# Thresholds and epsilon on another engine, shorter GpSimd pieces, paired V products, and a new order in a fused attention and two-layer expert kernel

## The chip, the cores and the metric

The kernel runs on one core of one Trainium2 chip. The metric is the device time of one execution in microseconds. A core has TensorE (matrix products, PE in the profile, with its weight loads apart as PEld), VectorE (DVE), ScalarE (ACT), GpSimd (POOL) and SyncE (SP), which issues most of the transfers. Each engine works through its own queue in order and waits there on semaphores of the others.

## The reference

```python
def _attn_ref(q, k, v, tau):                     # (4, 8, 576, 64) each
    scores = scale * np.matmul(q, k.transpose(0, 1, 3, 2))
    thresh = np.max(scores, axis=-1, keepdims=True) - tau
    scores = np.where(scores >= thresh, scores, -1000000000.0)
    attn = np.exp(scores - np.max(scores, axis=-1, keepdims=True))
    attn = attn / (np.sum(attn, axis=-1, keepdims=True) + 1e-09)
    return np.matmul(attn, v)
def _moe_ref(x, w_in, w_out):                    # (2304, 512), (512, 2048), (2048, 512)
    h = x @ w_in
    return (h - np.tanh(h)) @ w_out
def _moe2_ref(x, w_gate, w_output_gate, w1, w2): # 8 experts of 512 x 1024
    # each token goes to the expert of its largest logit:
    out[mask] = gate_w[mask, None] * eom[mask, e, None] * (np.maximum(x[mask] @ w1[e], 0.0) @ w2[e])
```

The attention's output, as 2304 tokens of 512, goes through the dense layer, and its result through the routed experts.

## The kernel before

The work has three stages. In the attention stage (0 to about 470 us) 32 units run one after another: 4 batches, two halves of the queries (`half` 0 with two tiles of 128 queries, `half` 1 with two and a merged third) and four pairs of heads. A unit is made of blocks of 128 queries by 576 keys, 144 in all. For a block TensorE makes the scores (L1085, or L1096 in the first eight units); VectorE copies them out of PSUM, negated and scaled, with their minimum (`em`, L1106); ScalarE makes the exponential (`e`, L1109); and VectorE masks it by the threshold, multiplies and sums in one instruction, the masked product (L1122, scalar_tensor_tensor with two inputs in SBUF). The threshold itself (`tb`, L1118) is one small addition of tau to the minima of a query tile, both heads at once. TensorE then transposes the block (L1138), ScalarE copies the transposes to `eth` and `elh`, and TensorE multiplies with V (L1193, half of the array's columns for each head), a burst of ten products for a unit, in two groups (`BURST`). The row sums `rs` get epsilon added (L1160) and are inverted (L1162), spread to `rb` (L1171, L1168), transposed into `rp`, and multiplied into the result `xf` (L1212). The high half of it, `xh`, is rounded on ScalarE or GpSimd (`round_to`) and the low half, `xl`, is a subtraction on GpSimd (`rest`).

Numbers are kept as a high and a low part in the format fp32r. `rest` makes all low parts: of K (`kst`), of q (`ql`), of the dense layer's weights (`wi`, `wo`, after the conversion from 64-bit numbers on L681 to L694), of the hidden values (`gl`), and of `xl`. On GpSimd a subtraction of more than `HALVE` = 400 columns is cut in two.

Steps of the dense layer (L743 into `ph`, L777 into `x`, with L756 to L766 between them) run beside the attention as soon as a chunk of 256 tokens is ready, and fill TensorE to about 720 us. The experts (L1750, L1637 and L1783) follow.

Buffers are rings: a tile of a tag with n buffers waits for the last use of the tile n before it. `EMN, EN, ETN, RBN` are the ring sizes of `em`, `e`, `eth` with `elh`, and `rb`.

The order of the instructions on each engine is set when the kernel is built. Every instruction is added to a planner with a duration in ns and a due time; `TAU` = 2600 ns is the due-time step of a block. In the main part the due times are replaced by a packed list of priorities, `URGENCY`, one for each instruction, and a greedy list schedule with the planned durations gives the order. The planner knows of a port that VectorE's instructions marked `port=True` share with GpSimd's.

## Time and profile before

| | before |
|---|---|
| time, median of 3 runs | 970.16 us (969.92 to 971.55) |
| the profiled execution | 971.04 us, of which the span of instructions is 969.2 |
| TensorE busy | 940.4 us (97%) |
| VectorE busy | 727.5 us (75%) |
| ScalarE busy | 551.1 us (57%) |
| GpSimd busy | 346.0 us (36%) |
| mean granted TensorE clock | 0.998 |

Busy time is the union of an engine's instructions; an instruction that waits for a resource after its start counts as busy. Matrix products are pipelined, and their recorded ends are modelled, so a busy TensorE isn't one at its peak. In a row of a group stand the line, the engine, the operation, the tiles written and read, the shapes, the count, then the busy time in us, the mean length in ns, the idle time of the engine just before these instructions in us, and what ended it.

### The profile page before, as it was taken

The page shows a single profiled execution, that of the slowest core. Times are in us where ns is not written, and L with a number is a line of the kernel's source. Part 1 is how long each engine was busy: PE and PEld are TensorE (multiplying, and loading weights), DVE is VectorE, ACT ScalarE, POOL GpSimd, SP SyncE. Part 2 cuts the span into 40 slices and gives each one's busy share as a digit, 9 for nine tenths or more (in the row PEclk, how much of TensorE's full clock was granted, in tenths as well). Part 3 has the DMA queues.
Part 4 walks back from the last instruction along what each step waited for, and adds up shares of the span by engine and source line. Part 5 has one row for each costly group of instructions (what it writes and reads, how often), then busy time and mean ns, then how long its engine had stood idle before and what let it go on. Part 6 is the DMA issues. An engine that isn't in the chain of part 4 may idle for free.

```text
span 969.2 us, 18499 instructions
## 1 busy us (share of the span) xinstructions
PE 940.4 (97%) x6636; PEld 806.5 (83%) x6636; DVE 727.5 (75%) x1812; ACT 551.1 (57%) x1142; POOL 346.0 (36%) x434
## 2 busy tenths in 40 slices
PE   8899889999999999999999999999999999999996
PEld 4556667888888888888899888888888899999996
DVE  7999999898789877857268668888676777646630
ACT  5888777777778767757445444344343434435421
POOL 1368548884667754434210101011012302213101
PEclk9999999999999999999999999999999999999999
DMA  9264645565664662451595366476854876655600
GB/s 268 102 204 150 195 139 183 170 206 169 198 215 160 193 244 86 132 182 45 180 364 175 118 189 158 130 169 137 266 177 144 271 229 229 193 169 165 214 14 32
DMA packets 71604, 168.70 MB, mean 174 GB/s; under 512 B 32382, under 2 KB 33022, under 8 KB 65616
## 3 DMA queue, kind: packets, MB, share of 16 engines
q1 hardware_dynamic: 67872, 157.41, 51.3%
q0 software_dynamic: 3200, 9.77, 2.9%
q8 instruction: 54, 0.88, 0.4%
q14 instruction: 46, 0.38, 0.1%
q10 hardware_dynamic: 432, 0.26, 0.1%
HBM read 125.99 MB, written 35.45 MB: 167 GB/s over the span
## 4 chain that ended last, share of the span: by engine, by line
PE 81%; DVE 14%; issue 2%; ACT 1%; DMA 1%; POOL 0%; POOLq 0%; DVEq 0%; ACTq 0%
PE x L777 20%; PE ph L743 20%; PE ph L1750 9%; PE py L1637 8%; PE sp L1085 5%; PE pv L1193 5%; DVE em L1122 5%; PE pt L1138 4%; DVE em L1106 3%; PE py L1783 2%; DVE ct L691 1%; PE pt L1682 1%; PE ph L1388 1%; DVE ct L694 1%; DVE tb L1118 1%
## 5 line engine op out<-in xcount | busy, mean ns | idle before, releaser
L743 PE MATMUL ph<-xh,wi 128*128 128x256 f32 x1152 | 178.1, 286 | 1.2 <-DVE u L766 1.1
L777 PE MATMUL x<-wo,gh 128*128 128x512 f32 x576 | 167.7, 404 | 0.0
L743 PEld LDWEIGHTS ph<-xh,wi 128*128 128x128 f32 x1152 | 156.3, 188 | 10.4 <-DVE u L766 3.1
L1122 DVE SCALAR_TENSOR_TENSOR em<-em,tb,e 128x576 f32<-128x576 f32 x144 | 142.4, 1003 | 8.0 <-ACT e L1109 5.0
L1109 ACT ACTIVATE e<-em,mx 128x576 f32<-128x576 f32 x144 | 110.8, 774 | 46.1 <-DVE em L1106 43.3
L1106 DVE TENSOR_SCALAR_CACHE_REDUCE em<-sp 128x576 f32<-128x576 f32 x144 | 107.6, 749 | 36.9 <-PE sp L1085 31.0
L556 POOL TENSOR_SCALAR gh<-u 128x512 fp32r<-128x512 f32 x52 | 38.4, 739 | 220.2 <-DVE u L766 168.5
L777 PEld LDWEIGHTS x<-wo,gh 128*128 128x128 f32 x576 | 99.0, 189 | 16.4 <-issue 1.3
L756 ACT ACTIVATE u<-ph 128x512 f32<-128x512 f32 x72 | 43.0, 598 | 94.2 <-PE ph L743 89.9
L764 DVE SCALAR_TENSOR_TENSOR w<-w,u 128x512 f32<-128x512 f32 x72 | 53.9, 748 | 53.6 <-ACT w L760 53.3
L743 PE MATMUL ph<-xl,wi 128*128 128x256 f32 x576 | 93.5, 284 | 0.0
L1138 PE MATMUL pt<-ident,em 128*128 128x128 f32 x576 | 84.3, 276 | 7.6 <-DVE em L1122 5.2
L554 ACT ACTIVATE eth<-pt 128x512 f32<-128x512 f32 (+1 forms) x160 | 84.6, 548 | 12.5 <-PE pt L1138 11.7
L777 PE MATMUL x<-wo,gl 128*128 128x512 f32 x288 | 90.6, 401 | 0.0
L1138 PEld LDWEIGHTS pt<-ident,em 128*128 128x128 f32 x576 | 65.6, 141 | 22.9 <-ACT eth L554 6.5
L743 PEld LDWEIGHTS ph<-xl,wi 128*128 128x128 f32 x576 | 79.6, 189 | 1.0
L1085 PE MATMUL sp<-kst,qh 128*128 128x288 f32 (+2 forms) x252 | 73.7, 311 | 2.9 <-DVE em L1106 2.8
L1193 PE MATMUL pv<-eth,vt 128*64 128x256 f32 (+1 forms) x512 | 71.6, 414 | 0.9 <-ACT elh L554 0.9
L1619 POOL DMA_INDIRECT out_dram<-o,ids x23 | 24.4, 1059 | 130.9 <-ACT o L1615 127.6
L1755 ACT ACTIVATE hh<-ph 128x320 fp32r<-128x320 f32 (+2 forms) x56 | 22.7, 420 | 83.2 <-PE ph L1750 82.9
L574 DVE TENSOR_TENSOR w<-wraw,w 128x512 fp32r<-128x512 f32 x98 | 65.5, 688 | 5.7 <-ACT w L554 4.3
L1085 PE MATMUL sp<-kst,ql 128*128 128x288 f32 (+2 forms) x252 | 68.0, 293 | 0.0
(380 smaller groups left out, 2003.7 us busy)
## 6 DMA issues: line engine op xcount, KB each, us to landing
wraw<-in_w_dram SPq DMA_DIRECT2D x60, 512.0 KB, 4.5
wi<-wsv SPq DMA_DIRECT2D x17, 1024.0 KB, 5.8
wo<-wsv SPq DMA_DIRECT2D x17, 1024.0 KB, 6.2
craw<-in_w_in_dram SPq DMA_DIRECT2D x14, 512.0 KB, 5.1
craw<-in_w_out_dram SPq DMA_DIRECT2D x14, 512.0 KB, 3.8
kr<-in_kT_dram SPq DMA_DIRECT2D x24, 288.0 KB, 4.6
wsv<-wi SPq DMA_DIRECT2D x6, 1024.0 KB, 4.6
wsv<-wo SPq DMA_DIRECT2D x6, 1024.0 KB, 5.9
```

The lines of the kernel that those rows point to most:

```text
L554: return sc.add("ACT", act(n, psum), due, lambda: nc.scalar.activation(dst(), src(), AF.Copy), r, w)
L574: return sc.add(eng, dve(n, psum) + 5 if eng == "DVE" else pool_tt(n), due, lambda: e.tensor_tensor(out=dst(), in0=src(), in1=hi().bitcast ...
L743: nc.tensor.matmul(ph.t[:, j, :], wi.t[:, w_, cc * CH + j * P:cc * CH + (j + 1) * P], x_.t[:, cc, :], start=(n == 0 and cc == 0), stop=(n ...
L777: nc.tensor.matmul(x2b[c, half][t].t, g_.t[:, j, t * P:(t + 1) * P], wo.t[:, w_, j * DM:(j + 1) * DM], start=(first and n == 0 and j == 0) ...
L1085: nc.tensor.matmul(sp.t[:, kb_, o:o + w], q_.t[:, q0:q0 + P], kb.t[:, hh, c0:c0 + w], start=(i == 0), stop=(i == len(todo) - 1),)
L1106: sc.add("DVE", 665, d, lambda ev=ev, sp=sp, mx=mx: nc.vector.tensor_scalar(out=ev().rearrange("p (a b) -> p a b", a=2), in0=sp.t[:, :, 0: ...
L1109: sc.add("ACT", 667, d + 800, lambda e=e, ev=ev, mx=mx: nc.scalar.activation(e.t, ev(), AF.Exp, bias=mx(), scale=-1.0), [(em, h), (m2, h)] ...
L1122: sc.add("DVE", 729, d + TAU, lambda ev=ev, tb=tb, e=e, col=col: nc.vector.scalar_tensor_tensor(out=ev(), in0=ev(), scalar=tb(), in1=e.t, ...
L1138: nc.tensor.matmul(pt.t[:, kt, :], em.t[:, c0:c0 + P], ident, is_transpose=True, start=(kt == 0), stop=(kt == 3))
L1193: nc.tensor.matmul(pvf()[h * D:(h + 1) * D], vb_.t[:, k, :], eth[h].t[:, kt, 0:n] if kt < 4 else elh.t[:, 0:n], start=(kt == 0), stop=(kt ...
L1637: nc.tensor.matmul(py[k].t[:, 0:cap], wx()[:, k * P:(k + 1) * P], x_.t[:, 0:cap], start=(f == 0 and n == 0), stop=(f == 7 and n == 2))
L1750: nc.tensor.matmul(ph.t[:, 0:cap], wx()[:, cc * P:(cc + 1) * P], x_.t[:, cc, 0:cap], start=(n == 0 and cc == 0), stop=(n == 2 and cc == 3))
```

## The change

- `thr` and `eps` go from "D" to "A": the 80 thresholds and the 32 epsilon additions are ScalarE's (activation Identity with a bias) and no longer VectorE's.
- `rest` on GpSimd cuts a subtraction into pieces of at most 144 columns (`FINE`) where its due time is before 150 us (`FINE_T`), and of at most 288 after that.
- `products` is a new function that issues the V products and all that follows them. For `half` 0 of batches 2 and 3 it is called once for two units: their twenty products are one instruction group on TensorE, into two halves of one PSUM bank. All other units call it alone.
- The ring of `e` has 2 buffers in place of 3, and that of `rb` 5 in place of 3.
- The planner's durations of some instructions change (335 to 343 for L685 and L688, 602 to 607, 665 to 678, 729 to 745, 400 to 570 and the like), which changes no instruction, and the list `URGENCY` is another one.

```diff
@@ -47,10 +47,13 @@
 ROUNDS = 24
 PORT = True
 HOLD = 160
-HALVE = 400
+HALVE = 288
+FINE = 144
+FINE_T = 150e3
 FULL = 8
 EARLY = 4
-EMN, EN, ETN, RBN = 5, 3, 2, 3
+EMN, EN, ETN, RBN = 5, 2, 2, 5
+PAIRED = 2
 BURST = (3, 2)
 WARMUP = 9
 NHH = 12
@@ -61,8 +64,8 @@
 ENGINES = {
     "conv_h": "A", "conv_l": "P", "conv_lb": "D", "ga_h": "P", "ga_l": "PPPD", "gb_h": "DP", "gb_l": "D", "k_h": "A",
     "k_l": "P", "q_h": "A", "q_l": "P", "p_h": "A", "p_l": "D", "p_h2": "A",
-    "x_h": "AP", "x_l": "P", "w_h": "AD", "w_l": "D", "w_l0": "D", "f_h": "A", "thr": "D", "eps": "D", "r_2": "DA",
-    "r_3": "PD", "clamp": "D", "bot": "A", "sum": "D",
+    "x_h": "AP", "x_l": "P", "w_h": "AD", "w_l": "D", "w_l0": "D", "f_h": "A", "thr": "A", "eps": "A", "r_2": "DA",
+    "r_3": "PD", "clamp": "D", "bot": "A", "sum": "D", "xm": "D",
 }
 LAG = {
     ("ACT", "DVE"): 150, ("ACT", "PE"): 260, ("ACT", "POOL"): 172, ("DVE", "ACT"): 130, ("DVE", "PE"): 256,
@@ -560,15 +562,17 @@
 
     def rest(cls, n, due, dst, src, hi, r, w, psum=False):
         eng = pick(cls) if cls in ENGINES else cls
-        if eng == "POOL" and n > HALVE:
+        if eng == "POOL":
+            np_ = -(-n // (FINE if due < FINE_T else HALVE))
+
             def part(k):
                 a, b, h_ = dst(), src(), hi().bitcast(F32)
                 m = a.shape[1]
-                cut = slice(0, (m + 1) // 2) if k == 0 else slice((m + 1) // 2, m)
+                cut = slice(m * k // np_, m * (k + 1) // np_)
                 nc.gpsimd.tensor_tensor(out=a[:, cut], in0=b[:, cut], in1=h_[:, cut], op=ALU.subtract)
 
-            for k in range(2):
-                o = sc.add("POOL", pool_tt(n // 2) + 110, due, lambda k=k: part(k), r, w)
+            for k in range(np_):
+                o = sc.add("POOL", pool_tt(n // np_), due, lambda k=k: part(k), r, w)
             return o
         e = nc.vector if eng == "DVE" else nc.gpsimd
         return sc.add(eng, dve(n, psum) + 5 if eng == "DVE" else pool_tt(n), due, lambda: e.tensor_tensor(
@@ -1115,11 +1119,11 @@
                 sc.add("ACT", 187, d + 801, lambda m2=m2, t2=t2, nt=nt: nc.scalar.activation(
                     t2.t[:, 0:nt], m2.t[:, 0:nt], AF.Identity, bias=tau_t), [m2, tau_m], [t2])
             else:
-                sc.add("DVE", 75, d + 801, lambda m2=m2, t2=t2, nt=nt: nc.vector.tensor_scalar(
+                sc.add("DVE", 133, d + 801, lambda m2=m2, t2=t2, nt=nt: nc.vector.tensor_scalar(
                     out=t2.t[:, 0:nt], in0=m2.t[:, 0:nt], scalar1=tau_t, scalar2=None, op0=ALU.add), [m2, tau_m], [t2])
             for h, d, mx, tb, ev, e in tl:
                 col = 4 if merged else 2 * h + qt
-                sc.add("DVE", 729, d + TAU, lambda ev=ev, tb=tb, e=e, col=col: nc.vector.scalar_tensor_tensor(
+                sc.add("DVE", 745, d + TAU, lambda ev=ev, tb=tb, e=e, col=col: nc.vector.scalar_tensor_tensor(
                     out=ev(), in0=ev(), scalar=tb(), in1=e.t, op0=ALU.is_le, op1=ALU.mult,
                     accum_out=rs.t[:, col:col + 1]), [t2, e], [(em, h), (rs, col)], port=True)
             dl = d
@@ -1157,15 +1161,15 @@
             sc.add("ACT", 200, ds, lambda: nc.scalar.activation(
                 rs.t[:, 0:nr], rs.t[:, 0:nr], AF.Identity, bias=eps_t), (), [rs])
         else:
-            sc.add(eng, 75 if eng == "DVE" else 220, ds, lambda: e_.tensor_scalar(
-                out=rs.t[:, 0:nr], in0=rs.t[:, 0:nr], scalar1=1e-9, scalar2=None, op0=ALU.add), (), [rs])
-        sc.add("DVE", 81, ds, lambda: nc.vector.reciprocal(out=rs.t[:, 0:nr], in_=rs.t[:, 0:nr]), (), [rs])
+            sc.add(eng, 110 if eng == "DVE" else 220, ds, lambda: e_.tensor_scalar(
+                out=rs.t[:, 0:nr], in0=rs.t[:, 0:nr], scalar1=1e-9, scalar2=None, op0=ALU.add), (), [rs], port=True)
+        sc.add("DVE", 92, ds, lambda: nc.vector.reciprocal(out=rs.t[:, 0:nr], in_=rs.t[:, 0:nr]), (), [rs])
         rbs = []
         for qt in range(2 + half):
             rb = buf("sm", "rb", RBN, [P, P])
             rbs.append(rb)
             if qt == 2:
-                sc.add("POOL", 400, ds + 260, lambda rb=rb: nc.gpsimd.tensor_scalar(
+                sc.add("POOL", 570, ds + 260, lambda rb=rb: nc.gpsimd.tensor_scalar(
                     out=rb.t, in0=blk, scalar1=rs.t[:, 4:5], scalar2=None, op0=ALU.mult), [rs], [rb])
             else:
                 sc.add("ACT", act(P), ds + 260, lambda rb=rb, qt=qt: nc.scalar.activation(
@@ -1181,50 +1185,77 @@
         round_to("p_h2", n, dl + 500, lambda: elh.t[:, 0:n], lambda: plf()[:, 0:n], slots, [elh], True)
         if half:
             round_to("p_h2", D, dl + 500, lambda: elh.t[D:P, 256:320], lambda: plf()[D:P, 320:384], slots, [elh], True)
-        xf = buf("ep", "xf", 2, [P, 320])
-        dl += TAU
+        waiting.append((ui, dl + TAU, eth, elh, rbs))
+        if half or b < PAIRED or hp % 2:
+            products(waiting)
+            del waiting[:]
+        return dl + 5 * TAU
+
+    waiting = []
+
+    def products(todo):
+
+        dl = todo[-1][1]
         pv = buf("ps_v", "pv", 1, [P, 4, P])
-        pvf = lambda: pv.t.rearrange("p a b -> p (a b)")[:, 0:n]
...
+        xfs, runs = [], []
+        for i, (ui, _, eth, elh, rbs) in enumerate(todo):
+            b, half, hp = units[ui]
+            n = 320 if half else 256
+            vb_ = vts[b, hp]
+            pvf = lambda i=i, n=n: pv.t.rearrange("p a b -> p (a b)")[:, 256 * i:256 * i + n]
+
+            def pairs_(kts, pvf=pvf, vb_=vb_, eth=eth, elh=elh, n=n):
+                for kt in kts:
+                    for h in range(2):
+                        nc.tensor.matmul(
+                            pvf()[h * D:(h + 1) * D], vb_.t[:, 2 * kt + h, :],
+                            eth[h].t[:, kt, 0:n] if kt < 4 else elh.t[:, 0:n], start=(kt == 0), stop=(kt == 4))
+
+            k0_ = 0
+            for g in BURST if len(todo) == 1 else ():
+                sc.add("PE", (538 if half else 432) * g, dl, lambda k0_=k0_, g=g, pairs_=pairs_: pairs_(range(k0_, k0_ + g)),
+                       [vb_] + [elh] * (k0_ + g == 5) + eth, [(pv, i)], mode=1)
+                k0_ += g
+            runs.append((pairs_, [vb_, elh] + eth))
+            if len(todo) > 1 and i:
+                sc.add("PE", 432 * 10, dl, lambda: [f(range(5)) for f, _ in runs],
+                       [x for _, r in runs for x in r], [(pv, 0), (pv, 1)], mode=1)
+        for i, (ui, _, eth, elh, rbs) in enumerate(todo):
+            b, half, hp = units[ui]
+            n = 320 if half else 256
+            pvf = lambda i=i, n=n: pv.t.rearrange("p a b -> p (a b)")[:, 256 * i:256 * i + n]
+            xf = buf("ep", "xf", 2, [P, 320])
+            xfs.append(xf)
+            round_to("bot", n, dl + 1200, lambda xf=xf, n=n: xf.t[:, 0:n], pvf, [(pv, i)], [xf], True)
+        for (ui, _, eth, elh, rbs), xf in zip(todo, xfs):
+            b, half, hp = units[ui]
+            n = 320 if half else 256
+            d = dl + 2 * TAU
+            rp = buf("ps_v", "pv", 1, [P, 4, P])
+            rpf = lambda rp=rp: rp.t.rearrange("p a b -> p (a b)")
+            for qt, rb in enumerate(rbs):
+                if qt < 2:
+                    sc.add("PE", 109, d, lambda qt=qt, rb=rb, rp=rp: nc.tensor.transpose(rp.t[:, qt, :], rb.t, ident), [rb], [(rp, qt)])
+                else:
+                    sc.add("PE", 120, d, lambda qt=qt, rb=rb, rp=rp: nc.tensor.matmul(
+                        rp.t[:, qt, 0:D], rb.t, sel, start=True, stop=True), [rb], [(rp, qt)])
...
+                round_to("x_h", m, d + 1500, hi, src, [xf], [(xh, reg)])
+                rest("x_l", m, d + 1500, lambda xl=xl, r=r, m=m, hp=hp: xl.t[:, hp, r:r + m], src, hi,
+                     [xf, (xh, reg)], [(xl, reg)])
+                o += m
 
     starts = []
     k = 0
```

## Rows read from the trace of the kernel before

**Rows 1.** Stretches: PE, PEld, DVE, ACT, POOL busy us (instructions), granted clock, DMA.
```profile
0.00:160.00 160.00, 140.76 (x954) 93.14 (x955) 151.25 (x382) 122.55 (x246) 87.76 (x116) 1.00 0.55 172
160.00:480.00 320.00, 319.02 (x2267) 270.04 (x2266) 248.95 (x554) 227.29 (x471) 183.16 (x241) 1.00 0.51 168
480.00:740.00 260.00, 258.93 (x1878) 230.05 (x1877) 195.04 (x622) 113.32 (x238) 31.27 (x36) 1.00 0.62 185
740.00:970.00 230.00, 221.70 (x1543) 213.32 (x1542) 132.27 (x255) 87.90 (x188) 43.79 (x42) 0.99 0.53 171
```

**Rows 2.** Chain that ended last, by line, 0 to 160 and 160 to 480 us.
```profile
by line: DVE em L1122 27.6%; DVE em L1106 19.8%; issue 6.1%; DVE ct L691 5.4%; DVE ct L694 5.0%; DVE tb L1118 4.4%; DMA craw<-in_w_in_dram 4.0%; PE ph L743 3.6%; DVE ct L685 2.8%; PE pv L992 2.6%; DVE ct L688 2.5%; ACT e L1109 1.8%; PE pt L
...
by line: PE x L777 24.0%; PE ph L743 23.6%; PE sp L1085 16.2%; PE pv L1193 15.3%; PE pt L1138 11.3%; PE pv L1177 1.7%; PE pv L1208 1.2%; DVE em L1122 1.1%; issue 1.1%; DVE w L764 0.6%; PE pv L1210 0.5%; DVE em L1106 0.5%; ACT e L1109 0.5%; 
```

**Rows 3.** VectorE, groups by line and form, 0 to 160 us: busy, mean ns.
```profile
L1122 DVE SCALAR_TENSOR_TENSOR em<-em,tb,e 128x576 f32<-128x576 f32 x59 | 58.5, 997 | 0.9
...
L1106 DVE TENSOR_SCALAR_CACHE_REDUCE em<-sp 128x576 f32<-128x576 f32 x60 | 44.6, 747 | 5.0 <-PE sp L1096 4.8 <-PE sp L1085 0.2
...
L1118 DVE TENSOR_SCALAR tb<-mx,tau_t 128x2 f32<-128x2 f32 x27 | 9.7, 361 | 0.2
...
L685 DVE TENSOR_SCALAR ct<-ct 128x512 f32<-128x512 f32 x13 | 7.5, 576 | 1.0 <-ACT ct L681 1.0
...
L688 DVE TENSOR_SCALAR ct<-ct 128x512 uint32<-128x512 uint32 x13 | 7.4, 572 | 0.1
...
L1160 DVE TENSOR_SCALAR rs<-rs 128x4 f32<-128x4 f32 x8 | 1.8, 231 | 0.1
...
L1160 DVE TENSOR_SCALAR rs<-rs 128x5 f32<-128x5 f32 x5 | 1.5, 302 | 0.0
...
L1118 DVE TENSOR_SCALAR tb<-mx,tau_t 128x1 f32<-128x1 f32 x5 | 1.0, 197 | 0.0
```

**Rows 4.** VectorE, timeline at 55 to 58 us: start, length.
```profile
55.26 1.23 DVE L1122 SCALAR_TENSOR_TENSOR em<-em,tb,e 128x576 f32<-128x576 f32 x1
...
56.42 1.28 DVE L1122 SCALAR_TENSOR_TENSOR em<-em,tb,e 128x576 f32<-128x576 f32 x1
...
58.31 0.41 DVE L685 TENSOR_SCALAR ct<-ct 128x512 f32<-128x512 f32 x1
```

**Rows 5.** GpSimd, timeline at 55 to 58 us.
```profile
55.83 2.46 POOL L568 TENSOR_TENSOR ql<-qr,qh 128x256 fp32r<-128x256 f32 x2
```

**Rows 6.** Views of single lines: duration ns min/median/max; L574 from 0 to 160 us.
```profile
L1118 DVE TENSOR_SCALAR tb<-mx,tau_t x80: 178/228/910, 8.1 to 456.6; 128x2 f32<-128x2 f32 x64, 128x1 f32<-128x1 f32 x16
...
L1122 DVE SCALAR_TENSOR_TENSOR em<-em,tb,e x144: 785/851/1565, 8.4 to 457.4; 128x576 f32<-128x576 f32 x144
...
L568 POOL TENSOR_TENSOR wi<-ct,wi x24: 725/739/1317, 20.0 to 289.5; 128x256 fp32r<-128x256 f32 x24
...
L574 POOL TENSOR_TENSOR xl<-xf,xh x18: 316/734/1186, 28.3 to 157.6; 128x256 fp32r<-128x256 f32 x8, 128x64 fp32r<-128x64 f32 x7, 128x192 fp32r<-128x192 f32 x3
...
L906 ACT ACTIVATE eo<-og x9: 188/203/205, 582.4 to 728.1; 128x2 f32<-128x2 f32 x9
```

**Rows 7.** GpSimd, groups by line and form, 0 to 160 us.
```profile
L568 POOL TENSOR_TENSOR kst<-kr,kst 64x288 fp32r<-64x288 f32 x20 | 21.2, 1082 | 6.6 <-ACT kst L554 4.6 <-issue 1.4
L568 POOL TENSOR_TENSOR wi<-ct,wi 128x256 fp32r<-128x256 f32 x12 | 10.7, 909 | 20.9 <-ACT wi L554 20.8
```

**Rows 8.** TensorE, timeline around one burst of V products.
```profile
240.68 0.64 PE L743 MATMUL ph<-xl,wi 128*128 128x256 f32 x4
...
241.16 0.64 PE L743 MATMUL ph<-xh,wi 128*128 128x256 f32 x4
...
243.67 0.64 PE L743 MATMUL ph<-xh,wi 128*128 128x256 f32 x4
...
244.24 1.95 PE L1193 MATMUL pv<-eth,vt 128*64 128x256 f32 x16
...
246.55 1.09 PE L1138 MATMUL pt<-ident,em 128*128 128x128 f32 x8
```

More of the change, by code (lines that the diff above doesn't have):

```diff
@@ L412, in pool_tt @@
 def pool_tt(n):
-    return int(2.11 * n + (145 if n > 400 else 110 if n < 256 else 60))
+    return int(2.14 * n + 148)
 def mm(n, k=1):
@@ L1105, in attention @@
                     sc.add("PE", 1110 if merged else 528, d - TAU // 2, scores, [qh, ql] + kr_, [sp])
[L1106 removed]
+                sc.add("DVE", 678, d, lambda ev=ev, sp=sp, mx=mx: nc.vector.tensor_scalar(
                     out=ev().rearrange("p (a b) -> p a b", a=2), in0=sp.t[:, :, 0:288], scalar1=-0.125, scalar2=None,
@@ L1183, in attention @@
             round_to("p_h2", D, dl + 500, lambda: elh.t[D:P, 256:320], lambda: plf()[D:P, 320:384], slots, [elh], True)
-        xf = buf("ep", "xf", 2, [P, 320])
-        dl += TAU
-        pv = buf("ps_v", "pv", 1, [P, 4, P])
-        pvf = lambda: pv.t.rearrange("p a b -> p (a b)")[:, 0:n]
-        def pairs_(kts):
-            for kt in kts:
-                for h in range(2):
-                    k = 2 * kt + h
-                    nc.tensor.matmul(
-                        pvf()[h * D:(h + 1) * D], vb_.t[:, k, :],
-                        eth[h].t[:, kt, 0:n] if kt < 4 else elh.t[:, 0:n], start=(kt == 0), stop=(kt == 4))
@@ L1197, in attention @@
-        k0_ = 0
-        for g in BURST:
-            sc.add("PE", (538 if half else 432) * g, dl, lambda k0_=k0_, g=g: pairs_(range(k0_, k0_ + g)),
-                   [vb_] + [elh] * (k0_ + g == 5) + eth, [pv], mode=1)
-            k0_ += g
-        round_to("bot", n, dl + 1200, lambda: xf.t[:, 0:n], pvf, [pv], [xf], True)
-        dl += 2 * TAU
-        rp = buf("ps_v", "pv", 1, [P, 4, P])
-        rpf = lambda rp=rp: rp.t.rearrange("p a b -> p (a b)")
-        for qt, rb in enumerate(rbs):
-            if qt < 2:
-                sc.add("PE", 109, dl, lambda qt=qt, rb=rb: nc.tensor.transpose(rp.t[:, qt, :], rb.t, ident), [rb], [(rp, qt)])
-            else:
-                sc.add("PE", 120, dl, lambda qt=qt, rb=rb: nc.tensor.matmul(
-                    rp.t[:, qt, 0:D], rb.t, sel, start=True, stop=True), [rb], [(rp, qt)])
@@ L1212, in attention @@
-        sc.add("DVE", dve(n, True) + 5, dl + 400, lambda rpf=rpf: nc.vector.tensor_tensor(
-            out=xf.t[:, 0:n], in0=xf.t[:, 0:n], in1=rpf()[:, 0:n], op=ALU.mult), [rp], [xf])
-        t0 = b * S + half * 256
-        o = 0
-        while o < n:
-            c, r = divmod(t0 + o, CH)
-            m = min(CH - r, n - o)
-            xh, xl = chunk(c)
-            hi = lambda xh=xh, r=r, m=m: xh.t[:, hp, r:r + m]
-            src = lambda o=o, m=m: xf.t[:, o:o + m]
-            reg = (hp, r)
-            round_to("x_h", m, dl + 1500, hi, src, [xf], [(xh, reg)])
-            rest("x_l", m, dl + 1500, lambda xl=xl, r=r, m=m: xl.t[:, hp, r:r + m], src, hi,
-                 [xf, (xh, reg)], [(xl, reg)])
-            o += m
```

242 lines of the change are left out of this document (126 added, 116 removed).

## The prediction

> **What bounds the kernel now.** I read the table by stretches first, then the chain that ended last in the two halves of the attention stage, then the groups of VectorE and GpSimd in the first half, then single instructions there.
>
> The stretches [rows 1] show a kernel with two regimes. From 0 to 160 us VectorE is busy for 151.25 of 160 us and TensorE for 140.76. From 160 to 480 us TensorE is busy for 319.02 of 320 us, and VectorE for 248.95 only. From 480 us on TensorE stays the bound. The granted clock is 1.00 in the first three stretches and 0.99 in the last, so the clock is no term here.
>
> The chain [rows 2] agrees. In the first 160 us its largest lines are VectorE's: the masked product L1122 (27.6%), the eviction of the scores L1106 (19.8%), L691, L694, the threshold L1118 (4.4%), L685 and L688. Together these are 67.5%, and with the 6.1% of "issue", most of which lies between VectorE instructions, 73.6%. From 160 to 480 us the five largest lines are TensorE's (90.4%). What is taken off VectorE is therefore worth something in the first 160 us and next to nothing later, unless it lets TensorE's queue fill earlier.
>
> The VectorE groups [rows 3] carry a second message: instructions that do little take long. A threshold on 128x2 elements has a mean of 361 ns, and its shortest is 178 ns [rows 6]. The masked product has a mean of 997 ns against a shortest of 785. Two timelines of the same 3 us say why. GpSimd runs two subtractions of 256 columns from 55.83 to 58.29 us without a break [rows 5], and the masked product that starts at 56.42 takes 1.28 us [rows 4]. It ends at 57.70; counted back by 785 ns its work began at 56.9, about where the first of the two subtractions ends (57.06). GpSimd pays too: the two take 1.23 us each, where the median of 24 such pieces is 0.74 [rows 6]. The two engines take turns, one whole instruction at a time. Instructions that read PSUM don't show this: L1106 has a mean of 747 ns [rows 3].
>
> **The change part by part.** The sums are for the first 160 us. An instruction starts some 70 ns before the one ahead of it ends (55.26 + 1.23 = 56.49 against 56.42 [rows 4]), so 70 ns are taken off each mean.
>
> *Thresholds and epsilon.* Removed from VectorE: 27 x 0.291 + 5 x 0.127 us of thresholds and 8 x 0.161 + 5 x 0.232 us of epsilon additions [rows 3], 10.9 us. The bare work in it is 45 x (178 - 70) ns = 4.9 us [rows 6]; the other 6.0 us are turns waited for. Where the next VectorE instruction is a masked product, it takes over the wait, so the gain lies between 4.9 and 10.9 us. I take half of the waits: 7.9 us. The price is on ScalarE: 45 instructions at 200 ns, that of a 128x2 exponential [rows 6], are 9.0 us, which takes it from 122.55 to 131.6 of 160 us [rows 1]. That is not full, so I cost it at nothing. The cover is that the masked product waited only 0.9 us in this stretch for its exponential or anything else [rows 3]; without it, see the slower rival. Behind a threshold on ScalarE's queue stand the next exponential and the copy that empties the transposes' bank, for which TensorE waits. From 160 to 470 us the 67 other instructions leave an engine that is off the chain and join one that is busy 227.29 of 320 us: nothing.
>
> *Pieces of at most 144 columns.* The due-time limit of 150 us is some 57 blocks of 2.6 us in the planner's time; 59 masked products start before 160 us [rows 3], so the limit falls near there. In this stretch GpSimd ran 75 subtractions of 192 to 352 columns, in eight groups, of which two stand in [rows 7]. They become 153, 78 more. Between the shortest of 64 columns (316 ns) and the shortest of 256 (725 ns) lie 2.13 ns a column and a fixed 180 ns [rows 6]: an estimate of 14 us more GpSimd time, on 87.76 busy of 160 us [rows 1]. It fits, because most of its idle time there is waiting for ScalarE. What the pieces give VectorE: the waits on L1122 are 59 x (997 - 785) ns = 12.5 us and those on L685 and L688 26 x (574 - 410) ns = 4.3 us [rows 3, 4, 6], together 16.8. A piece half as long halves the wait of an instruction that meets one piece: 8.4 us. Where GpSimd has a backlog, as at 55 to 58 us, each turn is shorter and there are more of them, and the wait stays: 0. I take 4, nearer the backlog.
>
> The Trainium skill (SBUF — State Buffer, on the two sides of the memory) says that VectorE and GpSimd arbitrate for one port pair as an exclusive lock, held for the whole instruction, while the loser fully blocks. The timelines agree. By that rule alone the pieces would change the length of a turn and not their total, and this part would give nothing.
>
> *Later pieces.* After the limit, the bound of 288 columns makes three pieces of 235 out of two of 352; 512 columns stay two pieces and 576 stay two. This lies in TensorE's stretch, off the chain: nothing.
>
> *V products in pairs.* For the first halves of batches 2 and 3, eight units make four bursts instead of eight. A burst begins at 244.24 us, 0.57 after the four matmuls ahead of it began, where such fours follow each other in 0.48 [rows 8]: some 0.1 us lost at entry. What follows it starts 2.31 us later, its bare length. Four fewer: 0.4 us gained; bounds 0 and 0.8. A pair holds both buffers of eth and elh, so the next unit's copies out of the transposes wait for the burst. Its cover is the MoE work that fills TensorE there. Without it, each pair costs at most one burst of a unit, 2.3 us, 9 us in all; I take nothing. The outputs of a pair's first unit come later, but a chunk needs all four head pairs, so its stores and the MoE behind them on SP's queue don't move by it. None of the moved steps issues a DMA.
>
> *Rings.* Two buffers instead of three for the exponentials: an exponential now waits for the masked product two before it. The chain has 1.8% of 160 us on L1109 today [rows 2], 2.9 us; bounds 0 and another 2.9, and I take 1.
>
> *The order.* All instructions are put in a new order, and nothing in the trace prices this. What it can win at most is TensorE's idle time: 19.2 us before 160 us, 1.0 to 480, 1.1 to 740 and 8.3 after [rows 1]; it can lose as much. I take 0.
>
> **The sum.** VectorE is relieved by 7.9 + 4 = 11.9 us, of which the chain's 73.6% count: 8.8 us. Less 1 for the ring, plus 0.4 for the bursts: 8.2 us. The profiled execution took 971.04 us (a span of 969.2 and 1.8 around it), so it would take 962.8. It was 0.9 above the median of 970.16; against that the forecast is 962.
>
> **The rivals.** *The pieces give nothing.* The backlog rules, as at 55 us: 7.9 x 0.736 - 0.6 = 5.2 us gained, 965. Against it: many waits are single ones, since the median L1122 (851 ns) is far below the mean. The rule of the SBUF page speaks for this rival.
>
> *Both halves of the waits go.* 10.9 + 8.4 = 19.3 us, of which 14.2 count: 956. The order could add some of TensorE's waits, down to 952. For it: 19.2 us of TensorE's idle time lie in the stretch that gets relief.
>
> *No change.* The pieces make GpSimd late with the low halves of q and K and with the converted weights, and TensorE waits for those instead of for VectorE. Only the bare 4.9 us count, 3.6, and the ring takes back 2.9: 969.5. For it: the subtractions of K take 1082 ns each already [rows 7]. Against it: GpSimd is idle for 72 of 160 us.
>
> *Slower: ScalarE's queue.* A threshold needs both minima of its block, and stands on ScalarE behind whatever runs then, an exponential or a copy. Before, it was next to its user on VectorE. If each of the 32 thresholds makes the masked product behind it wait 0.6 us, this costs 19.2 us against 11.9 gained: 7.3 x 0.736 = 5.4 us slower, 975.5. It decides from 0.37 us a threshold on. For it: ScalarE is busy for 77% of the stretch and each result is needed at once. Against it: the product already waits for an exponential on the same engine, and loses 0.9 us in 160 by it.
>
> **The numbers.** The forecast has 0.42, pieces for nothing 0.15, the larger gain 0.17, no change 0.12, slower 0.14. Measurements of this kernel tell 0.2% from no change, 968.2 to 972.1. Faster is then 0.74, same 0.12 and slower 0.14. The range 953 to 971 leaves out the far end of the larger gain and most of the slower case, some 0.2. With forecast and the pieces for nothing alone it would be 959 to 966.
>
> **What would show it.** If the steps hold, the stretch that ends with the 59th masked product is some 9 us shorter, the mean of L1122 in it falls from 997 towards 930 ns, no instruction of the threshold's form is left on VectorE, GpSimd is busy for about 100 us of it, and the stage that TensorE bounds keeps its length but starts earlier. The forecast is wrong if VectorE's idle time ahead of L1122 grows by more than 10 us with ScalarE named as its releaser, if L1122's mean stays near 1000 ns, if the three stretches after 160 us change by more than 3 us in sum, or if TensorE waits for q, K or weights.

## The result, and the profile after

The changed kernel takes 958.83 us (median of four, 957.88 to 959.57) against 970.27 for the kernel before on the same chip: a ratio of 0.988, with an interval of 0.986 to 0.990, so 11.4 us faster. The forecast was 962, with 953 to 971. The profiled execution took 958.42 us with a span of 956.6, against 971.04 and 969.2; this pair is 12.6 us apart, 1.2 more than the medians.

The table by stretches of the changed kernel, columns as in [rows 1]:

```profile
0.00:160.00 160.00, 147.53 (x1024) 103.10 (x1025) 144.12 (x358) 137.77 (x310) 116.80 (x201) 1.00 0.58 183
160.00:480.00 320.00, 319.89 (x2287) 273.01 (x2286) 223.10 (x483) 234.06 (x532) 189.96 (x257) 1.00 0.53 180
480.00:740.00 260.00, 257.99 (x1848) 227.07 (x1847) 192.16 (x618) 110.75 (x237) 34.11 (x35) 1.00 0.59 173
740.00:957.00 217.00, 209.80 (x1485) 203.72 (x1483) 125.83 (x243) 83.87 (x179) 42.92 (x39) 0.99 0.52 169
```

The count in the first row is the one to read: 1024 matrix products are done in the first 160 us, where it was 954 [rows 1]. The 954th TensorE product of the changed kernel ends at 149.7 us instead of 160.3; the first 954 are nearly the same work in both kernels, and the first 3221 exactly the same. The gain is thus 10.6 us at this point; it is 13.5 at the 3221st product (467.1 against 480.6), 11.9 at the last (949.8 against 961.7) and 12.6 at the end of the span. Most of it is made in the first 160 us, and what follows, the stretch that TensorE bounds, keeps its length within 3 us, as the forecast had it.

VectorE in the first 160 us, groups by line and form, as in [rows 3] (the product L1122 is now L1126, the eviction L1106 is L1110, and L685 and L688 are L689 and L692):

```profile
L1126 DVE SCALAR_TENSOR_TENSOR em<-em,tb,e 128x576 f32<-128x576 f32 x62 | 55.4, 908 | 2.4 <-ACT tb L1119 2.1 <-ACT e L1113 0.2
L1110 DVE TENSOR_SCALAR_CACHE_REDUCE em<-sp 128x576 f32<-128x576 f32 x63 | 46.9, 748 | 7.7 <-PE sp L1100 5.9 <-PE sp L1089 1.4
...
L692 DVE TENSOR_SCALAR ct<-ct 128x512 uint32<-128x512 uint32 x14 | 7.7, 551 | 0.1
L689 DVE TENSOR_SCALAR ct<-ct 128x512 f32<-128x512 f32 x14 | 7.6, 540 | 2.6 <-ACT ct L685 2.5
```

The masked product's mean falls from 997 to 908 ns, the eviction, which reads PSUM, stays at 748, and no threshold is left on VectorE. Before this stretch's masked products VectorE now waits 2.1 us for thresholds from ScalarE. ScalarE and GpSimd, groups of the same stretch:

```profile
L1113 ACT ACTIVATE e<-em,mx 128x576 f32<-128x576 f32 x63 | 48.4, 772 | 7.8 <-DVE em L1110 5.1 <-DVE idm L515 1.3 <-DVE em L1126 1.2
...
L1119 ACT ACTIVATE tb<-mx,tau_t 128x2 f32<-128x2 f32 x28 | 8.1, 291 | 1.4 <-DVE em L1110 1.3
```
```profile
L572 POOL TENSOR_TENSOR kst<-kr,kst 64x144 fp32r<-64x144 f32 x32 | 21.0, 684 | 4.0 <-issue 2.4 <-ACT kst L556 1.0
L572 POOL TENSOR_TENSOR wi<-ct,wi 128x128 fp32r<-128x128 f32 x28 | 16.8, 626 | 24.1 <-ACT wi L556 24.1
```

A threshold on ScalarE takes 291 ns, not 200, and its wait for the minima is only 1.3 us. A piece of K's subtraction, of 144 columns, takes 684 ns where one of 288 took 1082 [rows 7]. Two timelines, VectorE's and GpSimd's around 60 us, show the turns, as [rows 4, 5] did:

```profile
60.51 1.00 DVE L1126 SCALAR_TENSOR_TENSOR em<-em,tb,e 128x576 f32<-128x576 f32 x1
```
```profile
60.28 0.62 POOL L572 TENSOR_TENSOR ql<-qr,qh 128x128 fp32r<-128x128 f32 x1
60.86 0.97 POOL L572 TENSOR_TENSOR gl<-u,gh 128x128 fp32r<-128x128 f32 x1
```

The product starts while the piece of q runs and takes 1.00 us, some 0.2 longer than the shortest product (773 ns in this kernel). In [rows 4] one that met a 256-column subtraction took 1.28. The next piece, of `gl`, then waits behind the product. By these rows the turns are still whole instructions; they have become shorter.

The chain of the first 160 us, by line, answers [rows 2]:

```profile
by line: DVE em L1126 11.2%; DVE em L1110 9.4%; PE x L781 7.4%; PE sp L1089 7.2%; issue 7.1%; PE pv L1210 6.6%; PE pt L1142 6.6%; ACT e L1113 5.0%; PE ph L747 4.8%; DMA kr<-in_kT_dram 4.5%; DMA tau_t<-in_tau_dram 3.9%; ACT eth L556 3.4%; AC
```

VectorE's two largest lines fall from 47.4% to 20.6%. TensorE, which had one line above 3%, has five above 4%: this stretch now hangs on both.

### The profile page after: what moved, and what is told of

Its sections match the earlier page's. It is cut to its first block, busy times and chain, and to the rows that moved or that the text cites. A ratio compares the mean times of both kernels' runs of the same rounds, so it can differ in the third digit from the quotient of the medians.

```text
span 956.6 us, 18593 instructions
## 1 busy us (share of the span) xinstructions
PE 935.2 (98%) x6636; PEld 806.9 (84%) x6636; DVE 685.2 (72%) x1700; ACT 566.5 (59%) x1254; POOL 383.8 (40%) x530
## 4 chain that ended last, share of the span: by engine, by line
PE 75%; issue 11%; DVE 6%; ACT 3%; DMA 2%; POOL 2%; POOLq 0%; ACTq 0%; SPq 0%; DVEq 0%
PE x L781 20%; PE ph L747 20%; PE pv L1210 6%; PE sp L1089 6%; PE pt L1142 5%; PE ph L1781 4%; PE py L1668 4%; DVE em L1126 2%; PE py L1814 2%; DVE em L1110 2%; PE ph L1419 1%; POOL out_dram L1650 1%; ACT e L1113 1%; DMA kr<-in_kT_dram 1%; PE pv L1181 1%
## 5 line engine op out<-in xcount | busy, mean ns | idle before, releaser
L1126 DVE SCALAR_TENSOR_TENSOR em<-em,tb,e 128x576 f32<-128x576 f32 x144 | 134.6, 951 | 19.8 <-ACT tb L1119 15.9
L1110 DVE TENSOR_SCALAR_CACHE_REDUCE em<-sp 128x576 f32<-128x576 f32 x144 | 107.9, 751 | 36.6 <-PE sp L1089 30.1
L781 PEld LDWEIGHTS x<-wo,gh 128*128 128x128 f32 x576 | 98.4, 189 | 13.8
L572 POOL TENSOR_TENSOR ql<-qr,qh 128x235 fp32r<-128x235 f32 (+5 forms) x74 | 57.3, 796 | 20.2 <-ACT qh L556 18.1
```

Of the source, the lines that this page charges most:

```text
L572: nc.gpsimd.tensor_tensor(out=a[:, cut], in0=b[:, cut], in1=h_[:, cut], op=ALU.subtract)
L781: nc.tensor.matmul(x2b[c, half][t].t, g_.t[:, j, t * P:(t + 1) * P], wo.t[:, w_, j * DM:(j + 1) * DM], start=(first and n == 0 and j == 0) ...
L1110: sc.add("DVE", 678, d, lambda ev=ev, sp=sp, mx=mx: nc.vector.tensor_scalar(out=ev().rearrange("p (a b) -> p a b", a=2), in0=sp.t[:, :, 0: ...
L1126: sc.add("DVE", 745, d + TAU, lambda ev=ev, tb=tb, e=e, col=col: nc.vector.scalar_tensor_tensor(out=ev(), in0=ev(), scalar=tb(), in1=e.t, ...
```

## The experiments

The kernel before took 970.31 to 970.40 us beside them. In all but three of them the order of the kernel named is unchanged, and only what an instruction issues is another, so that order and edit come apart.

**The changed kernel with thresholds and epsilon back on VectorE.**

```diff
-                sc.add("ACT", 187, d + 801, lambda m2=m2, t2=t2, nt=nt: nc.scalar.activation(
-                    t2.t[:, 0:nt], m2.t[:, 0:nt], AF.Identity, bias=tau_t), [m2, tau_m], [t2])
+                sc.add("ACT", 187, d + 801, lambda m2=m2, t2=t2, nt=nt: nc.vector.tensor_scalar(
+                    out=t2.t[:, 0:nt], in0=m2.t[:, 0:nt], scalar1=tau_t, scalar2=None, op0=ALU.add), [m2, tau_m], [t2])
...
```

> The changed kernel with its thresholds and epsilon additions issued on VectorE again, each at the place that the new order gives it; all else, the order of every other instruction too, stays. My theory (VectorE's relief in the first 160 us is the cause, the thresholds' share 7.9 us at 73.6%) expects 5.8 us more than the changed kernel's 958.8: 964.6, between 962.4 (bare work alone) and 966.8 (all waits too). The rival that the new order brought the gain expects at most 960.5. The rival that ScalarE's queue makes thresholds late expects a faster kernel, under 957.

Measured: 963.63 us (962.80 to 963.99), ratio 0.993 [0.992, 0.994], so 4.8 us above the changed kernel and inside the expected 962.4 to 966.8. In its VectorE groups of the first 160 us the thresholds are back, and each takes 331 ns:

```profile
L1126 DVE SCALAR_TENSOR_TENSOR em<-em,tb,e 128x576 f32<-128x576 f32 x61 | 52.3, 873 | 1.3 <-ACT e L1113 0.2
L1119 DVE TENSOR_SCALAR tb<-mx,tau_t 128x2 f32<-128x2 f32 x28 | 9.2, 331 | 0.2 <-DMA tau_t<-in_tau_dram 0.2
```

The masked product is 35 ns shorter than in the changed kernel. That would fit the forecast's assumption, which counted half of the thresholds' waits: the threshold ahead of the product does part of the waiting for GpSimd. It isn't shown by itself, since GpSimd is also busy for less time here (110.81 us of the stretch against 116.80).

**The changed kernel with the old GpSimd pieces.** The last of the planned pieces that belong to one old piece issues that one whole.

```diff
-                cut = slice(m * k // np_, m * (k + 1) // np_)
-                nc.gpsimd.tensor_tensor(out=a[:, cut], in0=b[:, cut], in1=h_[:, cut], op=ALU.subtract)
+                old = 2 if n > 400 else 1
+                for j in range(old):
+                    if k == -(-(j + 1) * np_ // old) - 1:
+                        cut = slice(m * j // old, m * (j + 1) // old)
+                        nc.gpsimd.tensor_tensor(out=a[:, cut], in0=b[:, cut], in1=h_[:, cut], op=ALU.subtract)
```

> The changed kernel with GpSimd's subtractions merged to the pieces of before (512 and 576 columns in two, 704 in two, up to 320 whole), each merged piece at the place of the last of its parts; all else stays. My theory (4 us of waits at 73.6%) expects 2.9 us more than 958.8: 961.8. The rival that the pieces give nothing, since the port's total time stays, expects 958 to 959.5, and L1126's mean in the first 160 us near 908 ns. The rival that each wait is halved expects 965 and a mean near 1000 ns.

Measured: 961.27 us (960.26 to 961.59), ratio 0.990 [0.989, 0.992], 2.4 above the changed kernel, where 2.9 were expected. The masked product's mean is 935 ns, between the 908 and the 1000 that the two rivals named.

**Both undone: the new order, the pairs and the rings alone.** Both diffs above together.

> The changed kernel with both of these undone at once: thresholds and epsilon on VectorE, the pieces of before; the new order, the paired V products and the ring sizes stay. My theory expects 8.8 us more than 958.8, 967.6, so that order, pairs and rings are worth 2.6 us of the 11.4. The rival that the order brought the gain expects 959 to 961.

Measured: 969.55 us (968.48 to 971.22), ratio 0.9992 [0.998, 1.000]: no gain that can be told from nothing, and 2 us more than expected. The two edits together are worth 10.7 us in this order, more than 4.8 and 2.4 in sum. And the new order (with the pairs and the rings), which the forecast put at 0, is worth about that by itself. One row of this run changes how the masked product's mean is to be read:

```profile
L1129 DVE SCALAR_TENSOR_TENSOR em<-em,tb,e 128x576 f32<-128x576 f32 x59 | 52.5, 906 | 1.4 <-ACT e L1116 0.4
```

The old pieces and the old engine for the thresholds are back, and the mean is 906 ns all the same, as low as the 908 of the changed kernel. VectorE is nevertheless busy for 148.76 us of the stretch, only 2.5 less than before: other instructions got longer, the epsilon addition on 128x4 elements from 231 ns [rows 3] to 534. So the fall of this mean from 997 ns can't be put down to the pieces alone, and it gains no time by itself.

**The kernel before with both edits, in its own order.** If the forecast's reason was sufficient, this kernel should have had the gain. Its pieces are those of the changed kernel but for a few: 704 columns become six of 117 and not five of 141, for instance.

```diff
-                sc.add("DVE", 75, d + 801, lambda m2=m2, t2=t2, nt=nt: nc.vector.tensor_scalar(
-                    out=t2.t[:, 0:nt], in0=m2.t[:, 0:nt], scalar1=tau_t, scalar2=None, op0=ALU.add), [m2, tau_m], [t2])
+                sc.add("DVE", 75, d + 801, lambda m2=m2, t2=t2, nt=nt: nc.scalar.activation(
+                    t2.t[:, 0:nt], m2.t[:, 0:nt], AF.Identity, bias=tau_t), [m2, tau_m], [t2])
...
+        if eng == "POOL" and n > 144:
+            return sc.add("POOL", pool_tt(n), due, lambda: pieces(dst(), src(), hi().bitcast(F32), 0, n, due), r, w)
...
+    def pieces(a, b, h_, lo, hi_, due):
+        q = -(-(hi_ - lo) // (144 if due < 150e3 else 288))
...
```

> The kernel before, in its own order, with the thresholds and epsilon additions issued on ScalarE and the subtractions on GpSimd cut to at most 144 columns before the due time of 150 us and to at most 288 after; single bursts and old rings. My theory expects 8.8 us less than 970.2: 961.4. The rival that the order brought the gain expects 968 to 971. The rival of ScalarE's queue expects 972 to 976, since this order planned nothing on ScalarE at these places.

Measured: 972.86 us (972.30 to 975.57), ratio 1.003 [1.002, 1.004]. The expected 961.4 fell, and the rival of ScalarE's queue, which expected 972 to 976, named the time. The first two stretches of this kernel:

```profile
0.00:160.00 160.00, 144.77 (x965) 94.89 (x966) 135.82 (x341) 131.32 (x295) 109.10 (x193) 0.99 0.54 174
160.00:480.00 320.00, 316.22 (x2238) 266.48 (x2238) 225.24 (x480) 236.83 (x533) 191.45 (x270) 1.00 0.51 167
```

VectorE's busy time falls from 151.25 to 135.82 us, 15.4 us of relief, more than the 11.9 of the forecast. Yet TensorE does 965 products instead of 954 only: VectorE has become idle instead. Its waits in that stretch (what waited, for what; us in total, times, the longest):

```profile
DVE em L1130 <- ACT tb L1126: 7.9, 15, 1.1
DVE em L1114 <- PE sp L1104: 5.3, 3, 3.6
DVE ct L693 <- ACT ct L689: 3.6, 5, 1.1
DVE rs L1170 <- ACT rs L1168: 3.3, 6, 1.1
```

The same view of the changed kernel:

```profile
DVE em L1110 <- PE sp L1100: 5.9, 5, 4.2
DVE ct L689 <- ACT ct L685: 2.5, 4, 1.4
DVE em L1126 <- ACT tb L1119: 2.1, 6, 0.6
DVE em L1110 <- PE sp L1089: 1.4, 3, 0.9
DVE rs L1166 <- ACT rs L1161: 1.0, 1, 1.0
```

The waits for ScalarE (`tb`, `ct`, `rs`) are 14.8 us with the old order and 5.6 with the new one, which gets 3 more masked products done in the same time. ScalarE isn't the end of it. The chain that ended last, by line, in the first 160 us of the kernel before with both edits:

```profile
by line: POOL kst L565 5.7%; issue 4.9%; ACT e L1117 3.4%; POOL ql L565 3.2%; DMA kr<-in_kT_dram 3.1%; DVE em L1130 3.0%; POOL wo L565 3.0%; POOL gl L565 3.0%; POOL wi L565 2.8%; DVE em L1114 2.7%; ACT eth L554 2.0%; PE ph L751 2.0%; PE x L
```

It can be followed back to 67 us only. GpSimd's low halves are 17.7% of the 160 us, some 28 us, where the chain of the kernel before and that of the changed kernel have none in their largest lines ([rows 2] and above). So in the old order the longer GpSimd work is on the path as well.

The 954th product ends at 158.2 us, 2.1 earlier than before, but the 3221st at 483.0, 2.4 later. The relief did give a little time in the first stretch, and more was lost in the second, where TensorE is idle for 3.8 us against 1.0 before [rows 1]. The granted clock of 0.99 in the first stretch is worth some 1.6 us at full speed (0.01 x 160).

**The kernel before with one edit each.** The thresholds and epsilon alone, then the pieces alone, by the two parts of the diff above.

> The kernel before in its own order, with only the thresholds and epsilon additions issued on ScalarE. In the run with both edits in that order VectorE waited 7.9 us of the first 160 for thresholds. Theory now: the old order put each threshold behind an exponential on ScalarE and its product right behind it, so the edit needs another order; the run should be slower than before, 973 to 976. Rival: the pieces are what doesn't fit the old order (GpSimd late); then this run gains, 963 to 967.

Measured: 970.07 us (968.80 to 971.69), ratio 0.9997 [0.9988, 1.0006].

> The kernel before in its own order, with only the pieces on GpSimd made shorter (at most 144 columns before the due time of 150 us, at most 288 after). Theory: shorter turns need no other order, so it gains what undoing them in the new order cost, 2.4 us: 968. Rival: GpSimd gets late in the old order: 971 to 975. Rival that pieces give nothing: 970.

Measured: 970.73 us (968.54 to 973.00), ratio 1.0006 [0.9997, 1.0015]; the profiled execution is the fastest of them, 2.2 us under the median. Both expectations missed (973 to 976 and 968): neither is worth anything in that order. VectorE, ahead of its masked product, with the thresholds alone:

```profile
L1122 DVE SCALAR_TENSOR_TENSOR em<-em,tb,e 128x576 f32<-128x576 f32 x59 | 58.5, 997 | 6.9 <-ACT tb L1118 6.6
```

and with the pieces alone:

```profile
L1130 DVE SCALAR_TENSOR_TENSOR em<-em,tb,e 128x576 f32<-128x576 f32 x59 | 52.3, 893 | 0.9
```

The first gives VectorE 9.8 us (151.25 to 141.49 busy) and takes 6.6 back in waits for thresholds and 2.9 in waits for `rs`. The second shortens the product to 893 ns and VectorE's busy time by 6.7 us (to 144.60), with 23.5 us more GpSimd work (87.76 to 111.21). The chain of the second, by line, in the first 160 us, again followed back to 67 us only:

```profile
by line: DMA kr<-in_kT_dram 6.0%; DVE em L1130 5.3%; POOL wo L565 4.8%; DVE em L1114 3.9%; POOL gl L565 3.3%; ACT e L1117 3.3%; POOL kst L565 2.5%; issue 2.3%; ACT kst L554 2.3%; POOL ql L565 2.1%; POOL xl L565 2.0%; ACT w L768 1.6%; ACT et
```

GpSimd's low halves stand for 14.7% here, 23.5 us. The old order thus seems to lose the first edit's time at ScalarE and the second's at GpSimd; no run separates these.

**Thresholds moved up on ScalarE.** If a threshold is late only because it stands too far back in ScalarE's queue, the cure is to put each right behind the minima that it needs. Of 80, 69 move up in the order of the kernel before with both edits, and 67 in the changed kernel's, by one or two places. Nothing else is moved.

```diff
-        for o in self.order(rounds):
+        todo = self.order(rounds)
+        at = {o: k for k, o in enumerate(todo)}
+        todo.sort(key=lambda o: max(at[d] for d in o.deps | o.starts if d in at) + 0.5 if o.early else at[o])
+        for o in todo:
...
```

> The kernel before in its own order with both edits, and one thing more: each threshold stands on ScalarE right behind the minima that it needs, ahead of the exponential or copy that stood before it (69 of 80 move up by one or two places); all else keeps its place. If the place in ScalarE's queue is what cost the gain, most of the 7.9 us of waits in the first 160 go and the time falls from 972.9 to about 965. If the old order is at odds with the edits elsewhere, it stays within 2 us of 972.9.

> The changed kernel with the same shift: 67 of 80 thresholds move up on ScalarE to right behind their minima. There VectorE waits 2.1 us of the first 160 for thresholds, and the rest of its 15.9 us later, where TensorE sets the time. If the place is priced by the waits in the first stretch alone, it gains 0 to 1.5 us: 957.3 to 959. If the exponential that is passed over is then late, it is slower than 960.

Measured: 978.90 us (977.43 to 979.26, ratio 1.008 [1.007, 1.010]) for the kernel before with both edits, 6.0 worse than without the shift, and 970.33 us (968.73 to 972.22, ratio 1.000 [0.999, 1.001]) for the changed kernel, 11.5 worse. The expected 965 for the first fell; the second came out above 960, as expected for the case that the exponential passed over is late. ScalarE's waits, first 160 us, the kernel before with both edits and the shift:

```profile
ACT tb L1129 <- DVE em L1117: 11.5, 19, 1.6
ACT e L1120 <- DVE em L1117: 7.8, 9, 3.6
```

and the changed kernel with the shift:

```profile
ACT tb L1122 <- DVE em L1113: 13.4, 20, 2.0
ACT e L1116 <- DVE em L1113: 3.6, 1, 3.6
```

VectorE's wait for thresholds is smaller (7.9 to 2.7, and 2.1 to 1.6), but now ScalarE stands still in front of a threshold whose minima aren't there yet, with copies and exponentials queued behind it. The wait of 1.5 us in the changed kernel (both forms of the threshold) became 13.4, while that of the exponentials fell only from 5.1 to 3.6. The exponentials do come late: VectorE's waits for them rise from 3.5 to 12.4 us between 160 and 480 us, and TensorE's idle time there from 0.1 to 3.8. Too late stops VectorE, too early stops ScalarE, and one or two places decide which.

**The edits with the old priorities, planned anew.** The planner knows the new engines, lengths and pieces here, and only the list is the old one, carried over instruction by instruction.

```diff
-    'c-rk)_d`$Z8$SDU&S$lk22H7?5)mb36p4nUWxUB&B1*|B5lv;iDN@LmtVCtKlx*26WW33WdK13)efkr=zdC;K>73_0&;4BYbzk@O9Frw~v1JpM'
...
+    'c-rk)_d|}~|33E~&wie^mQg9QBqJGF6)L4fMw(PevLX^v%8HD<iwG$rqpa+a6$wdXuZ+yh<oh~zpa0<dtMmTht^0ZIb6(?mUDtJ<j42Tt@}5}U{#'
...
```

> The changed kernel with all its edits, but with the priorities of the kernel before carried over instruction by instruction (a piece has the priority of the subtraction it comes from), so that the planner makes a new order that knows the new engines and lengths, without the new list. If it is enough that the planner knows the new placement, the time is about that of the changed kernel, 957 to 962 us. If the list of priorities itself carries the gain, the edits come out no better than with the order of before: 970 us or more, up to 980.

Measured: 996.18 us (994.74 to 997.16), ratio 1.027 [1.025, 1.028]. That is 16 us beyond the 970 to 980 expected of this case. It isn't enough that the planner knows where an instruction runs. With the same edits the list alone moves the time by 37 us.

**Pieces of 72 columns, and short pieces throughout.** Each planned piece issues two halves, first in the early part alone, then after the limit alone.

```diff
-                cut = slice(m * k // np_, m * (k + 1) // np_)
-                nc.gpsimd.tensor_tensor(out=a[:, cut], in0=b[:, cut], in1=h_[:, cut], op=ALU.subtract)
+                q = 2 if due < FINE_T else 1
+                for j in range(q * k, q * k + q):
+                    cut = slice(m * j // (q * np_), m * (j + 1) // (q * np_))
+                    nc.gpsimd.tensor_tensor(out=a[:, cut], in0=b[:, cut], in1=h_[:, cut], op=ALU.subtract)
```

The second has `q = 2 if due >= FINE_T and n // np_ > FINE else 1`.

> The changed kernel with each early GpSimd piece cut in two again, at most 72 columns, at the same places of the order. If the wait of VectorE goes with the length of one GpSimd instruction, the masked product's mean in the first 160 us falls from 908 ns to about 860 and the time by some 2 us, to 957. If the total of the turns rules and each piece costs its fixed part of about 0.18 us, some 150 more pieces add 20 to 27 us of GpSimd time to 117 busy of 160, GpSimd's low halves come late, and the time goes up by 2 to 6 us, to 961 to 965.

> The changed kernel with the pieces after the limit of 150 us halved as well, at the same places of the order. TensorE bounds that part, so by the forecast's reading nothing changes: 958 to 960 us, with the first 160 us as they were. If VectorE's waits count there too, it is faster by 1 to 3 us, 956 to 958; if the longer GpSimd work makes its results late, slower by 1 to 3.

Measured: 980.88 us (979.27 to 982.19), ratio 1.011 [1.010, 1.013], with pieces of 72: 22 us worse than with 144, far beyond the expected 2 to 6. With short pieces throughout, 962.72 us (961.33 to 963.47), ratio 0.992 [0.991, 0.993], 3.9 worse than the changed kernel, where the forecast's reading expected no change: from 160 to 480 us GpSimd is busy for 215.97 us instead of 189.96, and TensorE, which bounds that stretch, is idle for 2.3 us instead of 0.1. The masked product with 72 columns, then four stretches of 20 us of that kernel and two of its waits between 60 and 140 us:

```profile
L1128 DVE SCALAR_TENSOR_TENSOR em<-em,tb,e 128x576 f32<-128x576 f32 x56 | 48.3, 879 | 4.1 <-ACT tb L1121 3.8
```
```profile
60.00:80.00 20.00, 17.59 (x117) 10.00 (x117) 14.23 (x33) 16.50 (x40) 19.60 (x50) 1.00 0.38 123
80.00:100.00 20.00, 17.37 (x115) 12.16 (x112) 13.74 (x34) 13.72 (x31) 19.45 (x52) 0.83 0.58 182
100.00:120.00 20.00, 15.47 (x105) 10.19 (x103) 16.73 (x41) 17.05 (x39) 19.76 (x47) 1.00 0.61 213
120.00:140.00 20.00, 15.33 (x92) 12.30 (x93) 12.27 (x32) 12.36 (x28) 18.09 (x51) 0.83 0.40 127
```
```profile
ACT ct L687 <- POOL wi L574: 4.9, 2, 3.0
PE x L783 <- POOL gh L558: 4.7, 1, 4.7
```

The product is shorter still, 879 ns on average, but GpSimd is busy for 76.9 of these 80 us. It was nearly full with 144 columns already, 73.0 us, but TensorE, VectorE and ScalarE hardly ever waited for it there: 0.4 us in all, for TensorE's weight loads. Now each of them is busy for less than 0.9 of the time, and ScalarE and TensorE wait for GpSimd, for 6.2 and 6.1 us; the largest of these waits are the two shown, for a low half (`wi`) and for a high half (`gh`) that GpSimd makes. Of the loss, 18.1 us are there by the 954th TensorE product (167.8 us against 149.7), so it falls in the stretch that GpSimd fills. In two of the four stretches the granted clock also falls to 0.83, a mean between TensorE's two levels of 1.2 and 2.4 GHz, after stretches in which TensorE was idle for 2.4 and 4.5 of 20 us. That is 0.17 x 20 = 3.4 us of full-speed work in each, at most 6.8 of the 22 us; how much of it counts wasn't measured.

**Three buffers for the exponentials.**

```diff
-            return pools[pname].tile(shape, dt, tag=tag, name=tag, bufs=n)
+            return pools[pname].tile(shape, dt, tag=tag, name=tag, bufs=3 if tag == "e" else n)
```

> The changed kernel with three buffers for the exponentials in place of two, at the same places of the order. The forecast put the smaller ring at a loss of 1 us, at most 2.9: the time would fall to 958 or, at the far end, 956. If the order is made for two buffers, no exponential is waiting for one, and nothing changes: 958.8 within 0.6.

Measured: 958.28 us (957.68 to 958.84), ratio 0.987 [0.986, 0.989], with a span of 956.7 against 956.6: the same. The ring of two costs nothing that can be measured.

The times by order and edit, in us; "new order" is with the pairs and the rings of the changed kernel:

| | nothing moved | thresholds, epsilon on ScalarE | shorter pieces | both |
|---|---|---|---|---|
| order of before | 970.3 | 970.07 | 970.73 | 972.86 |
| new order | 969.55 | 961.27 | 963.63 | 958.83 |
| old list, planned anew | | | | 996.18 |

## Why the prediction was right, and where it wasn't

**The place was right.** The forecast read two regimes and put the whole gain into the first 160 us. It was 10.6 us by the 954th TensorE product, against 8.2 forecast in all. After that the sums change by less than 3 us. Of the signs that the forecast named, one came out smaller: the 59th masked product ends at 151.6 us instead of 156.9, so 5.3 us earlier and not 9. Another would have misled: the mean of the masked product fell as announced, but the new order alone does that without gaining time. And VectorE does wait for thresholds from ScalarE, for 15.9 us in the whole attention stage; only 2.1 of these lie in the first 160 us, and the rest where TensorE sets the time.

**The relief of VectorE was right in kind, a little small in size.** Forecast: 7.9 for thresholds and epsilon and 4 for the pieces. Measured in the old order, where everything else stays: 9.8 and 6.7 separately and 15.4 together. The pieces were put nearer the case of a backlog, which gives 0. They turned out nearer the other bound, 8.4: with the order unchanged, the product's mean above its shortest of 785 ns [rows 6] went from 212 ns to 108, about half, as the forecast had it for products that meet one piece. The rival that the pieces give nothing is refuted for the new order: undoing them costs 2.4 us there and, with the thresholds back on VectorE, 5.9 (963.63 to 969.55). In the old order they do give no time, though VectorE is relieved. The Trainium skill (SBUF — State Buffer, on the two sides of the memory) describes the exclusive lock, and the timelines at 60 us agree with it (1.00 us for a product of 773 ns); what doesn't follow from it is that the total of the waits stays, and here it doesn't. The estimate of GpSimd's added work, 14 us, was too small: 23.5 in the old order. It counted no turns: a piece of 128 columns of `wi` takes 443 ns at the shortest in the changed kernel, and 626 on average in the first 160 us.

**ScalarE's price was too low and did hide.** A threshold takes 291 ns there, not the 200 of [rows 6], and the 48 moved instructions some 14 us, not 9. The exponential that gave the price reads no bias from a tile; the moved additions do. ScalarE is busy for 137.77 of 160 us and still isn't the bound.

**The terms don't add.** The forecast summed the relief ("of which the chain's 73.6% count") and the order ("I take 0"). Given the new order, both hold: the order, the pairs and the rings are worth 0.7 us, and the two edits then 10.7 where 8.8 were counted. Given the old order, neither does: the edits, with 15.4 us of relief, end 2.6 us slower, and the new order is then worth 14.0 (972.86 to 958.83). The chain's share says what the end hung on. It doesn't say what follows when one engine of the chain becomes faster while the queues of the others keep their order: here the freed time turned into waits, 13.8 of the 15.4 us into more waits of VectorE for ScalarE (14.8 against 1.0 before), and GpSimd came onto the chain. The edits make room, and only an order made for them uses it. That the sum came out within 3 us is in part luck, since the forecast didn't know that its first term hung on the term that it put at nothing.

The rival of ScalarE's queue could have warned. It decides "from 0.37 us a threshold on", counted over all 32 of the stretch. In the old order with both edits the waits for thresholds, 7.9 us, are 0.25 us each by that count (0.53 for each of the 15 that were waited for), so by thresholds alone it would not have decided. With the waits for ScalarE's `ct` and `rs` it is 14.8 us, or 0.46. So the mechanism is that rival's, VectorE waiting on ScalarE's queue, but it is wider than the threshold. In the changed kernel, whose order was made for the new engine, the thresholds' waits are 2.1 us.

**The rest.** The ring of `e`, put at 1 us lost, costs nothing. Epsilon wasn't separated from the thresholds. The pairs of V products were put at 0.4 us, less than these runs can tell; they were not undone by themselves, since another grouping needs another order, and what they give is open. The first pair is issued at 232.5 us of the changed kernel, so they have no part in what is gained before 160. The ring of `rb` with 5 buffers wasn't tested alone either. The argument that many waits are single ones compared the median of all 144 masked products (851 ns) with the mean of the first 59; of those 59 the median is 819 ns, which speaks for it more strongly. That the two edits undone together cost 10.7 us, 3.5 more than one by one, is measured, but which wait makes the difference isn't settled.

## What to carry to other kernels

In a kernel whose queues are ordered ahead of time, an edit that moves work between engines and the order that fits it are one change: price the order as the means by which the relief counts, not as a term beside it, and test an edit by itself only together with an order made for it. Moving a small instruction to an engine with free time is decided by its place in that engine's queue: one or two places earlier cost 6.0 and 11.5 us here. A mean that falls on the bounding engine isn't yet time gained. And shorter instructions on an engine that shares a resource paid here only while others didn't wait for that engine: 144 columns gained 2.4 us in the new order, and 72 lost 22.

## What was not expected of the hardware

ScalarE takes 278 to 309 ns for the addition of tau to 128x1 or 128x2 elements (median 288, 80 instructions), where an exponential of 128x2 elements in the kernel before takes 188 to 205 [rows 6], and VectorE's shortest threshold 178. The additions read their bias from a tile and the exponential has none; whether that is the difference, no run separates. A small instruction isn't free on a free engine. Halving a piece from 128 to 64 columns brought the converted weights' subtraction (`wi`) from a mean of 626 ns only to 383, so the same columns take 1.22 times as long on GpSimd, the turns waited for included.
